# Moving loads, casts and copies in the first third of a one-core retention + ELU feed-forward kernel

## The chip, the cores and the metric

The kernel runs on one core of one Trainium2 chip. The metric is device time in microseconds (us) of one execution. Before the change the median of three runs was 334.43 us (334.17 to 335.49). Each run comes with a state; all runs used here are of state fast, but for one, which is named where it comes up.

## The reference, cut to what matters

```python
# q, k, v: (8 batches, 8 heads, 576 positions, 64)
scores = matmul(q, k^T) / 8
ret    = scores * D          # D[i, j] = gamma_h ** (i - j) for i >= j, else 0
x      = matmul(ret, v)      # -> (4608 tokens, 512)
h      = x @ w_in            # 512 -> 2048
g      = where(h > 0, h, exp(min(h, 0)) - 1)     # ELU
out    = g @ w_out           # 2048 -> 512, float32
```

## The kernel before

The retention half works on *units*: unit u = 5b + r is a quarter of batch b (256 positions, four heads; r = 0 to 3) or the tail of that batch (r = 4: units 4, 9, 14, ...). A unit is loaded as float32 by the sync engine's DMA queue, cast to bf16 and scaled by the decay (`cast`), transposed (`turn_pe` on TensorE, PE, or `turn` by a DMA transpose in the sync queue), and used in a *stretch* of PE work. `ffn1` makes a tile of h and its ELU, `ffn2` a quad of four w_out matmuls. Units 5 to 9 are transposed on PE; from unit 10 on (the third batch) the DMA does it.

```python
def stretch(u, quick=False):          # p is the unit before u
    new_x()
    inter(p); scores(u); values(p); state(u)   # PE; scores(u) reads the transposed q and k
    ...                               # masks and prefix sums on VectorE, block diagonals on GpSimd,
                                      # copies of x on ScalarE

def cast_later(u):                    # chores: GpSimd's casts of u, then its DMA transpose
    cast(u, None, None)
    for i, e in ((1, 0), (1, 1), (0, 0), (0, 1)):
        chores.append(lambda i=i, e=e: cast_q(u, nc.gpsimd, i, (e,)))
    chores.append(lambda: cast_v(u, "p"))
    chores.append(lambda: turn(u))

sequence = [0, 1, 2, 3, 5, 6, 7, 8, 4] + list(range(9, NS))
def load_to(n): ...                   # issues the loads up to sequence[n] in the sync queue
# ... units 0 to 3, first tiles of the feed-forward ...
    values(2); put_x(2); drop(2)
    elu(0, 1, ph)                     # exp and relu on ScalarE, one step on VectorE
    put_end(2); put_end(3)
    for hl in range(2):               # the two halves of unit 3
        values(3, (hl,), st3)
        inter(3, (hl,), st3)
        put_x(3, (hl,), st3, ("ss", "sv")[hl])
        if hl == 0:
            ph = hidden(0, 2)         # PE: a feed-forward tile
# ... blocks 0 and 1 of the feed-forward; then (NU = 5, FT = 4):
for what in "q q q t q u t q u 7 q q t q u 8 f f t 4 f u f t 9 f u A f t f u f".replace(" ", ""):
    # q: ffn2 quad; t: turn_pe, u: stretch of units 5 6 7 8 4 9 in turn; f: ffn1 tile, then two chores
    if what == "7":
        cast(NU + 2, "p", "s"); load_to(NU + 3)     # q cast on GpSimd ("p"), v on ScalarE ("s")
    elif what == "8":
        cast(NU + 3, "p", "s"); load_to(NU + 4)
    elif what == "4":
        cast(FT); load_to(NU + 5)
    elif what == "9":
        cast(NU + FT); load_to(NU + 6)
    elif what == "A":
        cast_later(2 * NU)
stores()                              # four stores of output, issued by GpSimd
for u in range(2 * NU + 1, 2 * NU + 3):
    cast_later(u)
    load_to(u + 2)
def step(u):                          # one unit of the main loop
    chore(len(chores) - 6)
    stretch(u)
    load_to(u + 5)
    cast_later(u + 3)
```

## Time and profile before

| | before |
|---|---|
| median of runs | 334.43 us |
| profiled span | 332.1 us |
| PE busy in it | 305.2 us |
| longest wait of PE | 6.5 us, on one DMA transpose |

From the page of the kernel before, the span, the busy time of the engines, PE's busy share and PE's granted clock in 40 equal slices of 8.3 us (a 9 is 90% or more):

```profile
span 332.1 us, 8924 instructions
...
PE 305.2 (92%) x3570; PEld 206.3 (62%) x3613; DVE 202.9 (61%) x352; ACT 181.5 (55%) x354; POOL 175.0 (53%) x303
...
PE   7789986888399999999999999999999999999994
...
PEclk9999999999789999999999999999999999999999
```

PE is full from the twelfth slice on (91 us). Before it the row has holes, the deepest one a 3 in the eleventh slice, and there and in the next slice the clock row has a 7 and an 8.

### The profile page before, as it was taken

Reading aid. Unit: us, or ns where it says so; the run is one execution under the profiler, and the core shown is the slowest. Engines: PE = TensorE matmul, PEld = TensorE weight load, DVE = VectorE, ACT = ScalarE, POOL = GpSimd, SP = SyncE. Lnnn points to the kernel's source line nnn. Section 1 sums busy time; section 2 is a strip of 40 time slices with the busy share of each in tenths; the row PEclk is TensorE's granted clock in tenths of the full one; section 3 lists DMA queues with packets and bytes.
Section 4 is the critical chain, followed back from the end, with each engine's and each line's share of the span. In section 5 each row is a group of like instructions: output and inputs, shape, how many; then the busy total and the mean of one; then the engine's idle time right before and its main releaser. Section 6 shows DMA issues by size and latency. Waiting matters only on the chain.

```text
span 332.1 us, 8924 instructions
## 1 busy us (share of the span) xinstructions
PE 305.2 (92%) x3570; PEld 206.3 (62%) x3613; DVE 202.9 (61%) x352; ACT 181.5 (55%) x354; POOL 175.0 (53%) x303
## 2 busy tenths in 40 slices
PE   7789986888399999999999999999999999999994
PEld 2467643665356676666666666666676666666641
DVE  4758823588247677656775667576676776545530
ACT  3657454674155565555556556556565555665431
POOL 5927624698147957845568466936663832001000
PEclk9999999999789999999999999999999999999999
DMA  7999998039987994796756685856668410000102
GB/s 216 253 197 375 318 239 215 0 68 304 234 204 157 181 223 132 166 168 172 205 158 164 130 208 141 215 139 161 175 170 135 65 49 35 32 34 32 64 33 63
DMA packets 99037, 51.70 MB, mean 156 GB/s; under 512 B 43764, under 2 KB 93940, under 8 KB 98996
## 3 DMA queue, kind: packets, MB, share of 16 engines
q1 hardware_dynamic: 94740, 40.38, 53.7%
q0 software_dynamic: 4256, 10.75, 12.2%
q8 instruction: 28, 0.46, 0.6%
q14 instruction: 13, 0.11, 0.1%
HBM read 36.70 MB, written 9.44 MB: 139 GB/s over the span
## 4 chain that ended last, share of the span: by engine, by line
PE 79%; DMA 5%; POOL 4%; SPq 4%; issue 2%; ACT 2%; DVE 2%; POOLq 0%; DVEq 0%; ACTq 0%
PE ph L65 35%; PE pm L65 35%; PE x L65 5%; PE sc L65 3%; POOL qkn L195 2%; SPq L184 2%; DMA w_in_sb<-in_moe_w_in_dram 2%; DMA rqk<-in_k_dram 1%; DMA qkT<-qkn 1%; SPq L178 1%; ACT e L498 1%; ACT ot L521 1%; POOL s_mid L390 1%; ACT xt L364 1%; DVE em L507 1%
## 5 line engine op out<-in xcount | busy, mean ns | idle before, releaser
L65 PE MATMUL pm<-w_out_sb,g 128*128 128x512 bf16 x536 | 139.6, 380 | 3.5 <-ACT ot L521 1.3
L65 PE MATMUL ph<-xt,w_in_sb 128*128 128x256 bf16 x1024 | 133.7, 275 | 3.2 <-ACT xt L364 1.8
L498 ACT ACTIVATE e<-ph 128x512 f32<-128x512 f32 x144 | 86.1, 598 | 91.5 <-PE ph L65 91.4
L65 PEld LDWEIGHTS <-w_in_sb 128*128 128x128 bf16 x1152 | 110.1, 98 | 39.3 <-issue 3.5
L65 PEld LDWEIGHTS <-g 128*128 128x128 bf16 x576 | 56.2, 98 | 44.2 <-issue 2.4
L504 DVE SCALAR_TENSOR_TENSOR g<-e,ph 128x512 bf16<-128x512 f32 x73 | 50.2, 687 | 44.6 <-ACT ph L500 43.6
L507 DVE TENSOR_SCALAR em<-e 128x512 bf16<-128x512 f32 x71 | 41.0, 578 | 35.7 <-ACT e L498 35.6
L390 POOL TENSOR_TENSOR s_mid<-mid,diag 128x256 bf16<-128x256 f32 x32 | 19.5, 609 | 82.0 <-DVE mid L399 42.0
L508 DVE SCALAR_TENSOR_TENSOR g<-ph,em 128x512 bf16<-128x512 f32 x71 | 49.1, 692 | 7.7 <-PE ph L65 0.5
L500 ACT ACTIVATE ph<-ph 128x512 f32<-128x512 f32 x73 | 43.3, 593 | 0.0
L195 POOL TENSOR_TENSOR qkn<-rqk,gk 128x256 bf16<-128x256 f32 x64 | 39.9, 641 | 5.3 <-DMA rqk<-in_k_dram 5.1
L315 DVE TENSOR_TENSOR pt<-sc,mask 128x1024 bf16<-128x1024 f32 x31 | 37.7, 1217 | 6.4 <-PE sc L65 6.2
L364 ACT CAST xt<-x 128x256 bf16<-128x256 f32 x62 | 23.5, 450 | 29.4 <-PE x L65 25.1
L537 POOL DMA_DIRECT2D out_dram<-ot x31 | 17.8, 575 | 40.4 <-ACT ot L521 40.4
L195 POOL TENSOR_TENSOR qkn<-rqk,gq 128x256 bf16<-128x256 f32 x52 | 33.4, 656 | 0.1
L521 ACT COPY ot<-pm 128x512 f32<-128x512 f32 x36 | 21.1, 590 | 9.4 <-PE pm L65 9.4
L65 PE MATMUL sc<-qkT 64*64 64x128 bf16 (+1 forms) x576 | 16.1, 222 | 7.6 <-DMA qkT<-qkn 6.5
L390 POOL TENSOR_TENSOR s_end<-end,diag 128x256 bf16<-128x256 f32 x32 | 21.5, 671 | 2.6 <-DVE end L406 2.6
L65 PEld LDWEIGHTS <-qkT 64*64 64x64 bf16 x576 | 10.0, 107 | 13.0 <-DMA qkT<-qkn 6.7
L65 PE MATMUL ph<-xtt,w_in_sb 128*128 128x256 bf16 x128 | 16.6, 273 | 0.1
L240 POOL CAST vn<-rv 128x512 bf16<-128x512 f32 x24 | 15.6, 649 | 0.0
L265 ACT COPY qkT<-ptr 128x512 bf16<-128x512 bf16 x16 | 9.2, 591 | 10.1 <-PE ptr L264 10.1
(68 smaller groups left out, 170.9 us busy)
## 6 DMA issues: line engine op xcount, KB each, us to landing
rqk<-in_q_dram SPq DMA_DIRECT2D x32, 256.0 KB, 4.2
rqk<-in_k_dram SPq DMA_DIRECT2D x32, 256.0 KB, 4.2
rv<-in_v_dram SPq DMA_DIRECT2D x32, 256.0 KB, 5.1
out_dram<-ot POOLq DMA_DIRECT2D x31, 256.0 KB, 3.3
rqk<-in_moe_w_out_dram SPq DMA_DIRECT2D x16, 256.0 KB, 5.5
w_in_sb<-in_moe_w_in_dram POOLq DMA_DIRECT2D x2, 512.0 KB, 6.9
w_in_sb<-in_moe_w_in_dram POOLq DMA_DIRECT2D x1, 1024.0 KB, 8.9
rqt<-in_q_dram SPq DMA_DIRECT2D x8, 128.0 KB, 4.8
```

The lines of the kernel that those rows point to most:

```text
L65: pin(nc.tensor.matmul(*a, **kw))
L195: pin(eng.tensor_tensor(natt[u][0][:, i, e], x[:, e], g[:, e], ALU.mult))
L315: pin(nc.vector.tensor_tensor(pt.rearrange("p i h n -> p (i h) n"), sc.rearrange("p i (h n) -> p (i h) n", h=2), mask.rearrange("p k e r - ...
L364: pin(engines[eng[c]](dst.rearrange("p h (r e) -> p h e r", e=2), src))
L390: pin(eng.tensor_tensor(dst.rearrange("p h (j d) -> p h j d", j=2), src.unsqueeze(2).to_broadcast([P, 2, 2, D]), diag.unsqueeze(1).unsquee ...
L498: pin(nc.scalar.activation(e, ph, AF.Exp))
L500: pin(nc.scalar.activation(ph, ph, AF.Relu))
L504: pin(nc.vector.scalar_tensor_tensor(g, e, -1.0, ph, ALU.add, ALU.min))
L507: pin(nc.vector.tensor_scalar_add(em, e, -1.0))
L508: pin(nc.vector.scalar_tensor_tensor(g, ph, 0.0, em, ALU.max, ALU.min))
L521: pin(nc.scalar.copy(ot, pm))
L537: pin(eng.dma_start(out[r : r + P, :], ot))
```

## The change

The intent: the DMA transposes of the third batch should not queue behind loads that nobody needs yet; the casts of units 7 and 8 should be ready when PE asks for them; and a ScalarE copy that PE waits for should go ahead of an ELU that nobody waits for.

```diff
-    elu(0, 1, ph)
     put_end(2)
     put_end(3)
     for hl in range(2):
@@
         if hl == 0:
+            elu(0, 1, ph)
             ph = hidden(0, 2)
@@
-    for what in "q q q t q u t q u 7 q q t q u 8 f f t 4 f u f t 9 f u A f t f u f".replace(" ", ""):
+    for what in "q q q t q u 7 t q u 8 q t q u q f t 4 f u f t 9 f u A f t f u f f".replace(" ", ""):
         if what == "7":
-            cast(NU + 2, "p", "s")
+            cast(NU + 2, "v", "s")
@@
         elif what == "8":
-            cast(NU + 3, "p", "s")
+            cast(NU + 3, "v", "s")
@@
             cast(NU + FT)
-            load_to(NU + 6)
+            load_to(NU + 7)
@@
     for u in range(2 * NU + 1, 2 * NU + 3):
         cast_later(u)
-        load_to(u + 2)
+    load_to(2 * NU + 3)
@@ def step(u):
-        load_to(u + 5)
+        load_to(u + 4)
```

## The prediction

> **What bounds the kernel now.** I read the page first. TensorE (PE) is busy for 305.2 us of a span of 332.1 us, so at most some 27 us can be had without giving PE less work. To see where those 27 us lie I asked for busy time by stretch of the span (columns: stretch and its length, then busy us and instructions of PE, PE's weight loads, VectorE, ScalarE, GpSimd, then the granted clock, the DMA engines' share and GB/s):
>
> ```profile
> 51.60:54.70 3.10, 1.02 (x10) 0.47 (x10) 0.00 (x0) 0.59 (x1) 2.89 (x5) 1.00 1.03 285
> 54.70:58.00 3.30, 2.38 (x61) 1.55 (x60) 1.36 (x3) 2.21 (x5) 0.61 (x1) 1.00 0.76 202
> 58.00:62.00 4.00, 2.85 (x26) 1.91 (x24) 2.12 (x5) 2.67 (x6) 3.66 (x7) 1.00 0.00 0
> ...
> 81.40:87.90 6.50, 0.02 (x1) 0.00 (x0) 0.88 (x2) 0.00 (x0) 1.75 (x3) 0.90 1.18 209
> 87.90:92.00 4.10, 3.85 (x58) 2.80 (x60) 1.76 (x3) 1.68 (x4) 1.75 (x4) 0.50 1.22 291
> ```
>
> From 100 to 318 us PE is busy for over 99% of the time (99.27 of 100 us, then 117.10 of 118): that part is PE-bound and only moves as a block. The loss is in front of it. The waits of PE between 15 and 92 us (total us, times, longest) name the causes:
>
> ```profile
> PE sc L65 <- DMA qkT<-qkn: 6.5, 1, 6.5
> PE ptr L264 <- POOL qkn L195: 3.1, 7, 1.2
> PE ph L65 <- ACT xt L364: 1.3, 2, 0.9
> ```
>
> The first is one wait: the score matmuls of unit 11 want its transposed q and k (qkT), which a DMA transpose makes. The timeline of the sync engine's DMA queue (start, length, line, target and source) shows why it is late:
>
> ```profile
> 70.94 1.35 SPq L253 DMA_TRANSPOSE qkT<-qkn  x1
> 72.35 0.56 SPq L184 DMA_DIRECT2D rqk<-in_q_dram  x1
> ...
> 74.36 2.00 SPq L184 DMA_DIRECT2D rqk<-in_q_dram  x1
> ...
> 79.54 2.13 SPq L178 DMA_DIRECT2D rqt<-in_k_dram  x1
> 81.71 0.82 SPq L178 DMA_DIRECT2D rvt<-in_v_dram  x1
> 83.13 2.08 SPq L253 DMA_TRANSPOSE qkT<-qkn  x1
> ```
>
> Between the transposes of units 10 and 11 nine loads stand in the queue (units 12, 13 and 14). GpSimd has unit 11's q and k cast by 76.4 us (its timeline: the q part starts at 75.00 and takes 1.39 us), but the transpose is issued at 83.13 and lands 4.76 us later, at 87.89 (chain of waits). PE reached that point at 81.4. It waits on queue order, not on the cast.
>
> **What the Trainium skill says.** (1) "TensorE: Matmul & The Clock Gate", Part 1: The HAM clock gate: TensorE's clock falls to half after an idle window of about 3.4 us and comes back after about as much sustained work; its example falls 5.2 us after the last matmul. The trace agrees: PE stops at 81.4, the granted clock goes from 1.00 to 0.50 at about 86.5, stays 0.50 until about 93.2 and is 1.00 from 94. (2) "DMA: Bandwidth & Descriptors", Issuing engines are not separate DMA queues: all DMAs run on the same 16 engines and interleave, so taking a load out of the sync queue only helps a transpose by its place, and a load moved elsewhere still takes bandwidth. The trace agrees: in 72 to 84 us DMA share is 0.91 to 1.18, with the stores of GpSimd's queue among the loads. (3) "GPSIMD Engine Reference", 4.1 Engine selection: GpSimd is about 2x slower than VectorE at two-input elementwise work. Here the same cast with gq takes a median of 610 ns on GpSimd and 421 ns on VectorE (rows of rqk, 30 to 100 us): 1.45x, and the measurement decides.
>
> **The change, part by part.**
>
> *A. Loads and transposes.* Unit 12 is now loaded with unit 11, in the block of work that has its load at 51.6 to 53.2 us in the sync queue. The buffers for it are free by then (its q/k slot was last a w_out slot, cast before 38.4 us; its v slot belonged to unit 3). The DMA share is 0.00 to 0.01 from 58 to 72 us, so its 768 KB are free there. Behind the transpose of unit 10 only unit 13's three loads stand; unit 14's come after the transpose of unit 11. Later each step loads one unit less far ahead. Unit 11's transpose can then go as soon as its cast is done: on the old clock at 76.4, and with 4.76 us to land at 81.2, against PE's arrival at 81.4. So the wait of 6.51 us should shrink to 0 to 0.5 us. **Gain 6.5 us.**
>
> *B. The clock.* With no gap over 3 us PE stays at full clock. From 87.9 to 93.2 it ran at 0.50: 5.3 us x (1 - 0.50) = 2.65 us lost. Check: the score matmuls of unit 10 up to the fourth group of ffn matmuls after them take 75.22 to 79.30 = 4.08 us; the same list for unit 11 takes 87.93 to 94.72 = 6.79 us; difference 2.7. **Gain 2.7 us**, conditional on A.
>
> *C. Casts of units 7 and 8.* Their q and k casts (four of 0.6 us on GpSimd each) came right before PE's transposes of them:
>
> ```profile
> 52.86 0.29 PE L264 MATMUL ptr<-ident,qkn 128*128 128x128 bf16 x2 [1.22 <-POOL qkn L195]
> 53.43 0.28 PE L264 MATMUL ptr<-ident,qkn 128*128 128x128 bf16 x2 [0.28 <-POOL qkn L195]
> ...
> 57.78 1.69 PE L65 MATMUL ph<-xt,w_in_sb 128*128 128x256 bf16 x14 [0.92 <-ACT xt L364]
> ```
>
> PE ran them in pairs at the pace of GpSimd. The change emits each cast one stretch earlier and puts the q half on VectorE, which idles from 48.8 to 49.92 and from 51.5 to 56.6. Two VectorE casts take about 0.8 us (a pair at 9.62 took 0.76), so they fit the first gap; GpSimd's k half (1.2 us) ends about when its transposes come. Idle PE in 51.6 to 62.0 is 2.08 + 0.92 + 1.15 = 4.15 us (length less busy in the stretches above). In pairs eight transposes are busy 4 x 0.285 = 1.14 us, in one burst (at 44.96) 0.61: 0.53 more for each unit, 1.06 for two. The 0.92 wait on ScalarE's xt copy also goes, mostly: an ffn quad (0.86 us) now stands between unit 7's stretch and the first tile. In all 5.2 us. Against it: the two ScalarE copies of each transposed unit (1.07 to 1.10 us a pair, 0.6 more if an Exp is ahead) have one tile or quad of 0.87 us to hide behind, so I set 0.3 us for unit 7, 0.5 for unit 8 and 0.3 for the xt copy. **Gain about 4.1 us.** GpSimd also loses 4 x 0.6 = 2.4 us of work before units 10 and 11, so their casts move up with PE, and A's margin holds.
>
> *D. Copies ahead of the ELU of tile 1.* ScalarE ran exp and relu of that tile (20.66 to 21.77) before the first half-unit's copies:
>
> ```profile
> 21.14 0.63 ACT L500 ACTIVATE ph<-ph 128x512 f32<-128x512 f32 x1
> 21.66 0.50 ACT L364 CAST xt<-st 128x128 bf16<-128x128 f32 x2
> 21.80 0.69 DVE L504 SCALAR_TENSOR_TENSOR g<-e,ph 128x512 bf16<-128x512 f32 x1 [1.03 <-ACT ph L500]
> 22.04 0.47 PE L65 MATMUL st<-pt,vn 64*64 64x128 bf16 x8 [0.70 <-ACT xt L364]
> 22.83 0.30 DVE L364 CAST xt<-st 128x128 bf16<-128x128 f32 x1 [0.34 <-PE st L65]
> ```
>
> The 0.70 wait goes: copies at 20.8 to 21.3, PE's second half at 21.3. But exp and relu now end at about 22.25, and VectorE's ELU step of 0.69 us still stands ahead of its share of the last copy: 22.95, and the copy ends at about 23.25. PE's next tile started at 23.06, after copies that ended at about 23.1. The wait moves from in front of the second half to behind it. **Gain 0 us** (-0.2 to +0.3).
>
> Sum: 6.5 + 2.7 + 4.1 + 0 = 13.3 us; PE-bound work behind 92 us keeps the gain.
>
> **Rivals.** *R1: the transpose is still late.* With PE some 4 us earlier from C, unit 11's transpose must also come 4 us earlier. Were GpSimd's four stores (2.24 us of issue before unit 11's casts) or unit 13's load to hold it, a wait of 2 to 4 us would take the place of 6.5. For: DMA share was 1.0 right there, and some issues took 2.0 us instead of 0.55. Against: 768 KB + 384 KB of loads fewer ahead of it, and 2.4 us less on GpSimd. It makes about 324 to 326 us; below the clock's idle limit B still holds. *R2: loads are too late.* One unit less of lead: unit 15's load was issued at 85.25 and first cast at 102.69 (17 us); issued after the next transpose it would be at 88.75, still 14 us for a landing of 4 to 5 us. I give it under one in ten; each late load would cost a few us. *R3: VectorE becomes the bound in 47 to 52 us.* The cast of unit 7 fits a gap of 1.1 us by 0.3 us only; contention with GpSimd (one such cast took 0.83 us) would delay the prefix and mask of unit 6 by 0.2 to 0.4 us. Small: 0.5 us in all. *R4: ScalarE orders badly:* its v casts now stand ahead of the copies of unit 6 and wait for v of units 7 and 8 to land; v of unit 7 was issued at 40.05 and lands in 4.1 to 6.7 us, by 46.8, about when it is asked for. Up to 1 us.
>
> **Range and chances.** The sum gives 334.4 - 13.3 = 321.1; 0.5 us for R3 and R4 gives 321.6. The low end, 318.5, has all waits of C gone and the small ones after it too; the high end, 327.0, has R1 with C half lost. Faster by 2% means under 327.7, a gain of 6.7 us: A alone all but does it, and A with B does. So 0.91 faster, 0.08 within 2%, 0.01 slower.
>
> **What would show each step right or wrong.** A: in the waits of PE no qkT wait over 0.5 us, and three loads, not nine, between the first two DMA transposes. B: granted clock 1.00 from 60 to 120 us. C: no PE wait on qkn casts, PE at unit 8's stretch about 5 us earlier (one tile is moved behind it) and at unit 10's 4 us earlier. D: PE starts the tile after the last copies at 23.06, give or take 0.3. The prediction is wrong if a qkT wait of over 3.4 us remains (the clock then falls too), or if PE's idle time from 100 us on grows over the 1.6 us it has.

## The result, and the profile after

Ratios in this document are the mean time of one kernel's fast runs over that of the other's of the same rounds, so they are not quite the ratio of the medians quoted.

The first measurement gave 321.26, 324.64, 325.2 and 1736.15 us for the changed kernel against a median of 334.35 us before; the ratio of the fast runs is 0.9675 (95% interval 0.9591 to 0.9758). The profile fell on the execution of 1736 us, so it says nothing of the change. In it PE's matmuls differ from every other run, here those with w_out (instructions, then busy us and mean ns of one):

```profile
L65 PE MATMUL pm<-w_out_sb,g 128*128 128x512 bf16 x576 | 810.4, 1705 | 0.7 <-ACT ot L521 0.7
```

That row's mean is 380 ns in the profile before. From the start of four such matmuls to the start of the next group it took 5.29 us there and 0.86 us elsewhere, 6.1 times as long; from the start of a burst of 16 score matmuls to that of the next burst it took 0.81 us against 0.25. VectorE's mask operation kept its pace (1223 ns against 1217). The cause is open. The kernel was therefore run again.

**again** and **changed_3rd**, the changed kernel unaltered, on later chips.

> The changed kernel unchanged, because its first profile fell on an execution in which every matmul took about ten times its usual time. If that was a fault of that one execution, the profile shows a span of 319 to 324 us, and timed runs of 321 to 325.5 us, no score wait on a DMA transpose over 0.5 us if the prediction's step A holds. If the change itself brings on the slow state, one or more of these runs is far above 400 us again. If the rival R1 holds (the transpose of unit 11 is still late), a score wait of 1 to 4 us is there and the runs spread by more than 1%.

> The changed kernel once more, as the partner of the other three on one chip: 321.2 to 324 us, 0.962 to 0.965 of before, a transpose wait of 1 to 2 us, and none of the executions at five times the time.

| | before, same rounds | changed | ratio (95%) |
|---|---|---|---|
| again | 334.89 us | 321.83 us (321.19 to 323.89, 6 runs) | 0.9629 (0.9588 to 0.9670) |
| changed_3rd | 334.62 us | 322.34 us (321.27 to 323.01, 6 runs) | 0.9623 (0.9582 to 0.9663) |

None of these twelve executions was slow. From here "after" is the profile of again; the same rows of its page:

```profile
span 319.5 us, 8929 instructions
...
PE 302.4 (95%) x3569; PEld 205.0 (64%) x3613; DVE 203.6 (64%) x356; ACT 180.5 (57%) x354; POOL 173.1 (54%) x299
...
PE   8789998898999999999999999999999999999984
...
PEclk9999999999999999999999999999999999999998
```

The 3 is gone from PE's row, and the clock row has no dip where it had one. The waits of PE from 15 to 92 us, after (total us, times, longest):

```profile
PE sc L65 <- DMA qkT<-qkn: 1.5, 2, 1.3
PE ph L65 <- ACT xt L364: 1.1, 2, 0.6
PE ph L65 <- ACT qkT L265: 0.8, 1, 0.8
```

The wait of 6.5 us for a transpose has become 1.3 us (the other 0.2 is unit 10's), the 3.1 us on GpSimd's casts are gone, and 0.8 us on ScalarE's copies of a transposed unit are new. The sync queue, after (start, length):

```profile
66.15 1.35 SPq L253 DMA_TRANSPOSE qkT<-qkn  x1
67.55 0.56 SPq L184 DMA_DIRECT2D rqk<-in_q_dram  x1
68.16 0.92 SPq L184 DMA_DIRECT2D rqk<-in_k_dram  x1
69.12 1.00 SPq L184 DMA_DIRECT2D rv<-in_v_dram  x1
71.31 2.66 SPq L253 DMA_TRANSPOSE qkT<-qkn  x1
```

Three loads, not nine, stand between the transposes of units 10 and 11, and the queue was free 1.2 us before the second transpose: it now waits for its cast. The chain of waits shows what that transpose then took:

```profile
71.31 6.57 DMA qkT<-qkn
```

Before, the same piece took 4.76 us. The transposes of units 7 and 8 on PE, from PE's timeline after, with the tile behind unit 8's:

```profile
50.63 0.65 PE L264 MATMUL ptr<-ident,qkn 128*128 128x128 bf16 x8
...
55.20 0.61 PE L264 MATMUL ptr<-ident,qkn 128*128 128x128 bf16 x8
56.58 1.03 PE L65 MATMUL ph<-xt,w_in_sb 128*128 128x256 bf16 x8 [0.78 <-ACT qkT L265]
```

Each unit's eight transposes are one burst again, where before they came in pairs with a pause in front of each.

### The profile page after: what moved, and what is told of

The parts are those of the page before. It is cut to its first block, busy times and chain, and to the rows that moved or that the text cites. A ratio compares the mean times of both kernels' runs of the same rounds, so it can differ in the third digit from the quotient of the medians.

```text
span 1734.4 us, 8973 instructions
## 1 busy us (share of the span) xinstructions
PE 1727.8 (100%) x3613; PEld 699.3 (40%) x3613; DVE 202.7 (12%) x356; ACT 185.1 (11%) x354; POOL 165.9 (10%) x299
## 4 chain that ended last, share of the span: by engine, by line
PE 100%; ACT 0%; DVE 0%; issue 0%
PE pm L65 44%; PE ph L65 44%; PE x L65 7%; PE sc L65 3%; PE ptr L264 1%; PE st L65 1%; ACT ot L521 0%; DVE zero L74 0%
## 5 line engine op out<-in xcount | busy, mean ns | idle before, releaser
L65 PE MATMUL pm<-w_out_sb,g 128*128 128x512 bf16 x576 | 810.4, 1705 | 0.7 <-ACT ot L521 0.7
L65 PE MATMUL ph<-xt,w_in_sb 128*128 128x256 bf16 x1024 | 710.0, 1034 | 0.0
L65 PEld LDWEIGHTS <-w_in_sb 128*128 128x128 bf16 x1152 | 352.8, 309 | 496.8 <-issue 495.2
L65 PEld LDWEIGHTS <-g 128*128 128x128 bf16 x576 | 182.5, 317 | 399.0 <-issue 398.8
L65 PE MATMUL ph<-xtt,w_in_sb 128*128 128x256 bf16 x128 | 89.5, 1037 | 0.0
L65 PE MATMUL x<-pt,vn 64*64 64x128 bf16 x496 | 59.2, 673 | 0.0
L315 DVE TENSOR_TENSOR pt<-sc,mask 128x1024 bf16<-128x1024 f32 x31 | 37.9, 1223 | 148.8 <-PE sc L65 148.8
L65 PE MATMUL sc<-qkT 64*64 64x128 bf16 (+1 forms) x576 | 51.5, 576 | 0.0
L65 PEld LDWEIGHTS <-vn 64*64 64x64 bf16 x512 | 40.7, 288 | 3.2 <-issue 2.9
L65 PEld LDWEIGHTS <-qkn 64*64 64x64 bf16 x512 | 37.5, 293 | 1.3 <-issue 1.3
L65 PEld LDWEIGHTS <-s_end 128*128 128x128 bf16 x64 | 19.2, 317 | 41.0 <-issue 41.0
```

What stands on the lines that cost most here:

```text
L65: pin(nc.tensor.matmul(*a, **kw))
L315: pin(nc.vector.tensor_tensor(pt.rearrange("p i h n -> p (i h) n"), sc.rearrange("p i (h n) -> p (i h) n", h=2), mask.rearrange("p k e r - ...
```

## The experiments

**Three parts apart.** Each part was put alone on the kernel before.

**loads_only**, part A:

```diff
-            load_to(NU + 6)
+            load_to(NU + 7)
@@
-        load_to(u + 2)
+    load_to(2 * NU + 3)
@@
-        load_to(u + 5)
+        load_to(u + 4)
```

> Only part A: unit 12 loaded with unit 11, unit 14 after the transpose of unit 11, one unit less of lead. By the prediction's steps A and B: the 6.5 us wait shrinks to 0 to 0.5 us and the clock stays at 1.00, so 334.4 - 9.2 = 325.2 us. Rival: the transfers that go on in that stretch delay the transpose however it is queued, and 2 to 4 us of wait stay: 327 to 330 us with the clock kept, 330 to 332 if it still drops.

Measured: 327.12 us (326.34 to 328.07) against 334.89, ratio 0.9775 (0.9731 to 0.9819), about 7.5 us. PE's waits from 15 to 92 us:

```profile
PE ptr L264 <- POOL qkn L195: 3.1, 7, 1.2
...
PE sc L65 <- DMA qkT<-qkn: 1.5, 1, 1.5
```

The wait fell from 6.5 to 1.5 us, so 5.0 us of it and, with the clock, 2.7 more: 7.7 us. The time lies at the lower edge of the rival's range (327 to 330 us), the wait between the two theories (0 to 0.5 and 2 to 4 us): the queue's order was the larger part of it, and the rival holds for the rest. That rest is there without part C, so it is not a matter of PE having come earlier.

**casts_only**, part C:

```diff
-    for what in "q q q t q u t q u 7 q q t q u 8 f f t 4 f u f t 9 f u A f t f u f".replace(" ", ""):
+    for what in "q q q t q u 7 t q u 8 q t q u q f t 4 f u f t 9 f u A f t f u f f".replace(" ", ""):
@@
-            cast(NU + 2, "p", "s")
+            cast(NU + 2, "v", "s")
@@
-            cast(NU + 3, "p", "s")
+            cast(NU + 3, "v", "s")
```

> Only part C: casts one stretch earlier, their q half on VectorE, and the new order of quads and tiles. If C is worth 4.1 us in its place and the queue's nine loads simply move up with it: 330.3 us, the transpose wait still about 6.5 us. Rival: the transpose of unit 11 lands at the pace of the transfers, which do not move up, so that the wait grows by what C gains: 333 to 335 us, with a transpose wait of 9 to 11 us.

Measured: 330.16 us (328.43 to 332.56), ratio 0.9870 (0.9813 to 0.9926), 4.3 us by the ratio. From PE's timeline:

```profile
86.94 0.64 PE L65 MATMUL sc<-qkT 64*64 64x128 bf16 x16 [6.54 <-DMA qkT<-qkn]
```

The nine loads moved up with the rest, and the wait kept its 6.5 us and its half clock (0.64 us for a burst that takes 0.42 at full clock). The rival, a wait that grows by what C gains, is refuted. Parts A and C add up within their noise: 2.25% and 1.30% make 3.55%, against 3.71% and 3.77% for the whole change. But C's interval is wide (2.5 to 6.3 us), and this profile fell on the slowest of the four runs (332.56 us): its first tile waited 2.0 us for w_in and ran into half clock from 20.3 to 23.7 us, a trouble that comes up again below.

**elu_only**, part D:

```diff
-    elu(0, 1, ph)
@@
         if hl == 0:
+            elu(0, 1, ph)
             ph = hidden(0, 2)
```

> Only part D: the copies of the first half of unit 3 ahead of the ELU of tile 1. The prediction: nothing, 334.1 to 334.6 us, PE's next tile after the last copies at 23.06 give or take 0.3 us. Rival: the removed 0.70 us wait of PE counts in full, 333.7 us.

Measured: 335.03 us (333.66 to 336.36), ratio 1.0011 (0.9973 to 1.0050): nothing. Its timeline shows where the removed wait went:

```profile
22.23 0.66 ACT L500 ACTIVATE ph<-ph 128x512 f32<-128x512 f32 x1
...
22.75 0.36 ACT L364 CAST xt<-st 128x128 bf16<-128x128 f32 x1
...
22.92 0.69 DVE L504 SCALAR_TENSOR_TENSOR g<-e,ph 128x512 bf16<-128x512 f32 x1 [1.37 <-ACT ph L500]
23.16 0.49 PE L65 MATMUL ph<-xt,w_in_sb 128*128 128x256 bf16 x3 [0.58 <-ACT xt L364]
...
23.52 0.29 DVE L364 CAST xt<-st 128x128 bf16<-128x128 f32 x1
...
23.87 1.80 PE L65 MATMUL ph<-xt,w_in_sb 128*128 128x256 bf16 x15 [0.23 <-DVE xt L364]
```

PE no longer waits 0.70 us ahead of unit 3's second half. It waits 0.58 and then 0.23 us ahead of the next tile, where it waited 0.34 us before, since relu is now later, VectorE's ELU step waits for relu, and VectorE's copy stands behind that step. Unit 5's scores start 29.57 us after the first tile, against 29.56 before: nothing is left of the difference.

**before_warm: the clock alone.** The wait for the transpose stays; PE is kept busy through it.

```diff
 def stretch(u, quick=False):
     new_x()
+    if u == 2 * NU + 1:
+        warm(23)          # matmuls of zeros into a bank that is written over
     if late:
         inter(p)
```

> The kernel before, with 23 matmuls of zeros (about 0.216 us each at full clock, 5.0 us in all) put on PE ahead of unit 11's stretch, into a bank that is written over afterwards: the wait for the transpose stays, but PE is not idle through it. If the prediction's step B holds, the granted clock stays at 1.00 in 86 to 94 us and the kernel gains 2.7 us, 0.992 of before, with the end of the wait where it was. Rival: after the wait ScalarE and VectorE set the pace, and the half clock costs nothing: 1.000 of before.

Measured: 332.31 us (330.99 to 332.64) against 334.19, ratio 0.9929 (0.9904 to 0.9954): 2.4 us faster, with 23 matmuls more. The clock row of its page, then busy time by stretch (PE, weight loads, VectorE, ScalarE, GpSimd, clock, DMA share, GB/s):

```profile
PEclk9999998999999999999999999999999999999999
...
86.00:88.00 2.00, 1.69 (x10) 0.69 (x7) 0.00 (x0) 0.00 (x0) 0.00 (x0) 1.00 1.27 124
88.00:90.00 2.00, 0.64 (x48) 0.64 (x48) 0.16 (x1) 0.00 (x0) 0.00 (x0) 1.00 1.11 262
90.00:92.00 2.00, 2.00 (x32) 1.38 (x19) 1.55 (x3) 1.61 (x4) 0.59 (x2) 1.00 1.24 287
```

The clock stays at 1.00 where it was 0.50 before, and the kernel gains the 2.65 us that step B has, less 0.2, within the interval (1.5 to 3.2 us). In this profile the whole front lay 1.3 us later than in the profile before (unit 10's transpose was issued at 72.24 instead of 70.94), so the transpose landed at 89.3; the matmuls behind it ran at full clock. The 1.3 us come from the 8 in the clock row: the clock was at 0.50 from 55.2 to 58.6 us, behind PE's transposes of unit 7, which wait in pairs for GpSimd's casts. elu_only's profile shows the same (55.3 to 58.7 us), the profile of before does not. The rival, that another engine sets the pace there, is refuted.

**What holds the transpose that is left: stores_early and load13_later.** Both start from the changed kernel.

**stores_early:**

```diff
             cast(FT)
+            stores()          # in GpSimd's gap before unit 8's stretch, not after the whole list
             load_to(NU + 5)
```

> The changed kernel, with its four stores of blocks 0 and 1 issued from GpSimd's gap at 57.6 to 59.9 us (2.24 us, DMA engines nearly idle soon after) instead of at 66.6, ahead of unit 11's casts. If the 1.33 us wait left on unit 11's transpose is a matter of when its cast is done and of the stores' transfers, it goes to under 0.2 us: ratio to before 0.958 to 0.960 against 0.963 for the changed kernel. Rival: unit 13's load alone makes the transpose slow, the wait stays over 1 us: 0.962 to 0.964.

**load13_later:**

```diff
     for u in range(2 * NU + 1, 2 * NU + 3):
         cast_later(u)
-    load_to(2 * NU + 3)
```

> The changed kernel, with unit 13's load behind unit 11's transpose too, so that no load stands between the two transposes. If the load's transfers hold up the transpose (6.6 us from issue to landing against 4.5 as a median), the 1.33 us wait goes: 0.958 to 0.960 of before. Rival: the stores and the late cast hold it, and the wait stays over 0.7 us: 0.961 to 0.964; or the load now delays unit 12's transpose, with a wait there.

| | median | ratio to before (95%) | wait on qkT in its profile |
|---|---|---|---|
| again, changed_3rd | 321.83, 322.34 us | 0.9629, 0.9623 | 1.5, 1.5 us |
| stores_early | 320.65 us (319.79 to 322.69) | 0.9592 (0.9563 to 0.9621) | none |
| load13_later | 321.97 us (319.65 to 323.28) | 0.9611 (0.9571 to 0.9652) | 0.2 us |

Both take the wait away. So the remaining wait has two causes: with the load out of its way the transpose is fast enough though its cast comes no earlier (issued at 74.5 us, used at 79.7 without a wait, so it took at most 5.2), and with the stores out of the way unit 11's casts end 3.3 us after unit 10's transpose is issued instead of 5.1. That the load's transfers slow the transpose down follows from load13_later; how much of the 6.57 us is due to the stores' transfers is not told apart, since stores_early also brings the cast forward. load13_later's time is not clearly better than the changed kernel's, because three of its six runs were slower (323.2 to 323.3 us, mean clock 0.991). Its profile fell on one of them and shows another trouble, which the profiles of stores_early (322.69 us, 0.992), of pool_casts below (324.55 us) and of casts_only show too. From PE's timeline of stores_early:

```profile
18.55 1.61 PE L65 MATMUL ph<-xt,w_in_sb 128*128 128x256 bf16 x8 [1.73 <-DMA w_in_sb<-in_moe_w_in_dram]
```

The first piece of w_in came 1.73 us late (0.35 us in the profile after), the granted clock fell to 0.50 from about 19 to 22 us, and the first tile took 1.61 us instead of 1.05.

**stores_early_2nd**, the same kernel beside the changed one on one chip.

> The changed kernel with its first four stores in GpSimd's gap before unit 8's stretch, beside the changed kernel on one chip. If the transpose wait of 1.3 us was all it takes away: 1.0 to 1.4 us faster than the changed kernel, about 320.5 us. If the first gain (0.9592 against 0.9629, of different chips) was scatter: within 0.4 us of it.

Measured: 320.49 us (319.46 to 322.28), ratio 0.9572 (0.9532 to 0.9612), 1.85 us under changed_3rd by the medians and 1.5 us by the means. Its sync queue:

```profile
67.27 1.35 SPq L253 DMA_TRANSPOSE qkT<-qkn  x1
68.68 0.57 SPq L184 DMA_DIRECT2D rqk<-in_q_dram  x1
...
69.87 0.51 SPq L184 DMA_DIRECT2D rv<-in_v_dram  x1
70.97 1.23 SPq L253 DMA_TRANSPOSE qkT<-qkn  x1
```

Unit 11's transpose follows unit 10's by 3.7 us instead of 5.16, and no wait on qkT is left among PE's waits. The time gained is that of the wait removed. This version beats both kernels. With the intervals of the ratios overlapping a little, the case rests on the two measurements together and on the wait that is gone.

**stores_warm**, an attempt at the scatter:

```diff
+            stores()
@@
     turn_pe(3, "sv", 3, st[1])
+    warm(3, st[1])            # three more matmuls of zeros ahead of the first tile
```

> stores_early with three more matmuls of zeros (0.65 us) on PE ahead of the first ffn tile, where some executions wait 1.5 to 2 us for the first piece of w_in and then run up to 22 us at half clock. If that late piece and the clock drop are what sets the executions of 322.5 to 324 us apart from those of 320 to 321.5, the slow ones go and the fast ones lose about 0.2 us: all runs within 320 to 321.5 us. Rival: the piece comes late all the same, the clock still drops, and the scatter stays at 3 us.

Measured: 320.73 us (319.91 to 320.94, 5 runs), ratio 0.9567 (0.9528 to 0.9606). All runs lie within 1.0 us, as the first theory has it, and the mean is within 0.3 us of that of stores_early. But five runs are few: stores_early had one run of six above 321.5 us in each measurement. And changed_3rd had three runs of 322.6 to 323.0 us at a mean clock of 0.999 to 1.000, which a clock drop does not explain. What makes the rest of the scatter stays open.

**Which half of part C counts: pool_casts and old_order.** Both start from the changed kernel.

**pool_casts**, the new place with the old engine:

```diff
-            cast(NU + 2, "v", "s")
+            cast(NU + 2, "p", "s")
@@
-            cast(NU + 3, "v", "s")
+            cast(NU + 3, "p", "s")
```

> The changed kernel with the q casts of units 7 and 8 on GpSimd again, in their new places: what VectorE's share of part C is worth. GpSimd then needs 2.4 us a unit after s_end of units 5 and 6, until about 52.0 and 55.5 us, where PE's transposes ask at 50.6 and 55.2: waits on qkn of some 1.4 and 0.5 us, and the casts of units 10 and 11 up to 2 us later: 323.5 to 325.5 us, 0.967 to 0.973 of before. Rival: the place alone does it, and the engine does not matter: 0.962 to 0.964.

Measured: 322.26 us (321.92 to 324.55), ratio 0.9645 (0.9616 to 0.9673). My expectation of 323.5 to 325.5 us missed; the rival was nearly right. Its row of PE's waits:

```profile
PE ptr L264 <- POOL qkn L195: 0.5, 2, 0.3
```

**old_order**, the old place with the new engine:

```diff
-    for what in "q q q t q u 7 t q u 8 q t q u q f t 4 f u f t 9 f u A f t f u f f".replace(" ", ""):
+    for what in "q q q t q u t q u 7 q q t q u 8 f f t 4 f u f t 9 f u A f t f u f".replace(" ", ""):
```

> The changed kernel with the old order of tiles, quads and casts, but with the q casts of units 7 and 8 on VectorE: the engine alone. After pool_casts (the place alone keeps nearly all of part C, 0.9645) the theory is that the place counts: here the k casts on GpSimd still come right before their transposes, so PE waits on qkn for 1.5 to 2.5 us and on xt for 0.9 us again: 0.970 to 0.976 of before. Rival: halving GpSimd's burst by the use of VectorE is worth as much as the new place: 0.963 to 0.967.

Measured: 325.37 us (325.20 to 328.05), ratio 0.9724 (0.9683 to 0.9766). Its waits of PE:

```profile
PE ph L65 <- ACT xt L364: 2.0, 3, 0.9
...
PE ptr L264 <- DVE g L508: 1.3, 1, 1.3
...
PE ptr L264 <- DVE qkn L195: 0.8, 2, 0.5
...
PE ptr L264 <- POOL qkn L195: 0.5, 2, 0.3
```

The three waits of the transposes (ptr) add up to 2.6 us, and the wait on xt is back. The one that names g is the second half of unit 8's transposes: its k cast was done at 60.07 us, but the transposes began at 60.45, when VectorE's ELU step had ended at 60.39. In the program these transposes share three PSUM buffers with the tiles, and the old order has two tiles right ahead of them where the new one has one, so I take it for a wait on a buffer; no run tells that apart. The old order thus has two waits in store, and bringing the q half forward only uncovers the next. So by the ratios the new place, with its order of tiles and quads, is worth about 1 point (0.9724 against 0.9623) and the engine, given the place, 0.16 to 0.2, which is within the noise.

## Why the prediction was right, and where its terms were off

The prediction said 321.6 us; the two later measurements gave 321.83 and 322.34, and the first gave 324.92 with the slow execution among its four (324.64 without it). By its own steps, with the profiles of before and of again (332.1 and 319.5 us, 12.6 apart):

- **A, 6.5 us: the mechanism was right, the size was off.** loads_only shows that queue order was the cause. The failed term is "shrink to 0 to 0.5 us": 1.3 to 1.5 us remained (1.33 in this profile), so A was worth 5.2. I carried over the 4.76 us from issue to landing; with the load of unit 13 and four stores at work it took 6.57. That is the rival R1 at less than its stated 2 to 4 us, and the two causes that it names are the two found.
- **B, 2.7 us: right in size, by a rule that does not hold.** before_warm gave 2.4 us with nothing else changed; from unit 11's scores to unit 12's it took 8.74 us before and 6.13 after, 2.6 less. (In slices of 0.1 us the clock is 0.50 until about 93.45 us, not 93.2, so the step's first sum is 2.8.) But "with no gap over 3 us PE stays at full clock" is refuted: behind unit 7's transposes in before_warm no pause was over 1.22 us, and the clock fell. That the 1.3 to 1.5 us left of the wait kept the clock at 1.00 is what the profiles of again, changed_3rd and loads_only show; the rule did not assure it.
- **C, 4.1 us: right in kind, 0.7 too small.** Unit 10's score matmuls start at 70.40 us, 4.8 earlier than at 75.22, while the first tile starts alike (16.91 and 16.95). The 1.1 us of new waits that I set is what came: 0.27 us before unit 7's scores and 0.78 us after unit 8's transposes, both on ScalarE's copies, and nothing on xt in that stretch. What I left out is that the small waits behind them would go too: before, unit 4's score matmuls waited 0.65 us for ScalarE's copy (at 67.02) and a tile 0.25 us for g (at 69.01); after, neither is there. I credited VectorE with a part of the gain; by pool_casts and old_order the place, with its order of tiles and quads, earns nearly all of it. Neither the prediction nor this sum has the fall of the clock behind unit 7's transposes: with it unit 10's scores came 59.5 and 59.8 us after the first tile (before_warm, elu_only) instead of 58.3 (before). No profile of the new order has that fall, so in such executions C takes away 1.3 to 1.6 us more. How often they come is not shown.
- **D, nothing: right**, by the very sequence the prediction gave.
- **Sum:** 5.2 + 2.6 + 4.8 + 0 = 12.6 us, what the two spans differ by. A fell 1.3 us short, C made up 0.7 of it, and the 0.5 us set aside for R3 and R4, which did not come, covered the rest: that the total fits this closely is luck.
- **Rivals.** R2 did not come: no row of PE's waits over the whole span names a load of q, k or v. R3: VectorE's pair of casts took 1.17 us and not 0.8, beside GpSimd's pair at the same time (1.36 us instead of 1.18), yet unit 6's prefix started at 49.94 against 49.92 before. R4 did not show: the only new wait of PE in 46 to 54 us is C's 0.27 us.

On what was drawn from the Trainium skill: "TensorE: Matmul & The Clock Gate", Part 1: The HAM clock gate, carried step B, and before_warm agrees on what a long wait costs; on short ones see the last section. "DMA: Bandwidth & Descriptors", Issuing engines are not separate DMA queues, says that the transfers of all issuing engines interleave; I quoted it without pricing it. The 6.57 us fit it: load13_later shows the part of a load in the same queue, and no run tells the stores of GpSimd's queue apart. "GPSIMD Engine Reference", 4.1 Engine selection, led me to expect more of the change of engine than its 0.2% or so.

## What to carry to other kernels

When an engine waits for a transfer, look at what stands ahead of it in its own queue before looking at bandwidth; then price the transfers that remain beside it, because taking loads out of the queue does not take their neighbours off the DMA engines. A long wait of TensorE costs more than its length: here 6.5 us cost another 2.7 in half clock, so of several waits take the one that costs clock first, and look at the clock behind clusters of short waits too. And have an operand ready one stretch early rather than on a faster engine at the last moment.

## What the Trainium skill lacked or had wrong

- "TensorE: Matmul & The Clock Gate" (Part 1, and its advice to avoid idle gaps over about 3 us): a shorter gap can be enough. In stores_early PE stood idle from 16.83 to 18.55 us, 1.7 us, after 5 us in which it was busy nearly four fifths of the time (3.81 of 4.83 us), and the clock was 0.50 from about 19 to 22 us. pool_casts fell after a wait of 1.49 us at the same place; loads_only, with 1.50, kept a clock of 1.00 in 15 to 24 us. So the length of the gap alone does not decide. What goes with a fall in these profiles is how busy PE was over 3.41 us. The half-clock stretches last 3.41, 6.83 or 10.24 us (stores_early, before, elu_only). If the first 100 us of the seven profiles with a fall there are cut into pieces of 3.41 us, so that a piece ends where the clock fell, each of the nine falls follows a piece in which PE, as the profile counts it, was busy for 0.43 of the time or less. The other pieces at full clock have 0.48 or more, and the clock stayed. In loads_only, which has its only fall at the end of its run (323.8 us), the piece around the wait of 1.50 us has 0.56. No run was made to test this.
- No page tells of an execution with slow matmuls throughout (1736 us, one of the changed kernel's first four; 6.1 times as long for those with w_out, about three times for the scores) and the profile's clock row at 1.00.
- "DMA: Bandwidth & Descriptors" has no time from issue to landing for a DMA transpose of a 128 x 1024 bf16 tile beside other transfers: here 4.76 and 6.57 us for the same unit, with 4.5 us the median of 24 in the profile before.
- "GPSIMD Engine Reference", 4.1: about 2x slower than VectorE for two-input work; here 1.45x for a float32 multiply to bf16 (610 against 421 ns).
